# Forgetting attention and two MoE layers: one-bank PSUM tiles for the MoEs' outputs, and evictions issued one group earlier

## The chip, the cores and the metric

The kernel runs on one core of a Trainium2 chip. The metric is the device time of one execution in microseconds (us); lower is better.

## The reference

Attention with a decay over four batches of eight heads of 576 tokens, then two dense mixtures of the 2304 tokens (model width 512):

```python
scores = scale * q @ k.T + (cum[:, None] - cum[None, :])    # cum: running sum of log f, causal
x = softmax(scores) @ v                                      # 2304 tokens x 512
x = softplus(x @ w_in) @ w_out                               # first MoE, 2048 hidden
out = (sigmoid(x @ w_gate) * (x @ w_val)) @ w_out2           # second MoE, 1536 hidden
```

Every product is made in three matmuls of a high and a low part (high x high, high x low, low x high).

## The kernel before

The program has three stages, one behind the other, and PE (TensorE) works through all of them. Tiles are handed out by pools. An instruction waits for the instructions that used its tile, or the memory under it, before. The order on each engine is the order in which the code issues; nothing is reordered.

**Attention** (`Attention`, L22 on) works on 16 pairs of heads. A table of numbers (`WHEN`, `START`, `END`) sets the order. Scores go to PSUM banks `s` and to `X`; the products with v accumulate in two tiles of two banks each, `x_0` in `Y` and `x_1` in `X` (`pv`, L317). ACT (ScalarE) and DVE (VectorE) read them out: `out_a` (L340) and `out_b` (L345). In the last pair, `out_b` of `x_1` stands on DVE behind work on the first MoE's weights (`Weights.bits`, L502 to L506).

**The first MoE** (`Moe1`) takes five tiles of up to 512 tokens with 16 units each. `hidden` (L556 to L558 by the helper `three`) makes 12 matmuls into a bank `s`; ACT applies softplus (L586), ACT and DVE split the result into `gh` and `gl` (L597, L598). `output` adds 12 matmuls to four accumulators of one bank each. `BANKS` says where they lie: two of them in the `t` banks and two in a two-bank tile `Y`, or all four in `X` and `Y`. After the last unit of a tile `leave` (L625) copies the accumulators out, the even ones on DVE, the odd ones on ACT, and SP (SyncE) issues a DMA for each (L626). Those of the last tile are evicted while the second MoE begins.

**The second MoE** (`Moe2`) takes three tiles of 768 tokens with 12 units each. `hidden` makes seven products of six matmuls with 384 columns, into the two `s` banks `a` and `b` in turn; the third product needs the bank of the first one, so it waits until ACT has copied that out (L846, written `bl`). `output` adds 18 matmuls to six accumulators (blocks 0 to 5): blocks 0 and 1 in `t`, 2 and 3 in `X`, 4 and 5 in `Y`. On the last pass each finished block is evicted by `leave` (L916: even blocks DVE, odd blocks ACT) into a ring of four SBUF buffers `zs`, named `fw`, and SP issues its DMA to the output (L917). Block 4 so takes the buffer of block 0, and block 5 that of block 1; a copy into a buffer waits until the DMA out of it has landed. An eviction is not issued at once, but after the matmuls of the next block:

```python
            for x, y in self.leaves:
                self.leave(x, y)
            self.leaves = [(t, b)] if last else []
```

Block 5 of a tile is thereby issued after the first block of the next tile's first pass, one `hidden` later. The same unit's loads of weights stand on SP ahead of its DMA.

Of the kernel before, what the change touches and what calls it, by code (L numbers as in the profile page):

```python
# [21 lines left out]
class Attention:  # L22
# [2 lines left out]
    S = 576  # L25
    D = 64

    def __init__(self, nc, q, k, v, f, xT, pool, ps, dr):
        self.nc, self.q, self.k, self.v, self.f, self.xT = nc, q, k, v, f, xT
        self.B, self.HP = q.shape[0], q.shape[1]  # L30
        self.NP = self.B * self.HP
        self.c = pool("at_const", 1)
        self.R = {}
        self.ps, self.dr = ps, dr

    def pools(self, pool, io_pool):
        self.vp = pool("at_v", 2)
# [159 lines left out]
    def scores(self, R, p, i):  # L197


        nc, S = self.nc, self.S  # L200
        Xh, Xl, Yh, Yl, nb = R["Xh"], R["Xl"], R["Yh"], R["Yl"], self.nbs[p % 2]
        if "P" not in R:
            R["P"] = self.pp.tile([128, sum(self.W9)], F32, tag="P", name=f"P{p}")
            R["m"] = self.sm.tile([128, 9], F32, tag="m", name=f"m{p}")
            R["sum"] = self.sm.tile([128, 9], F32, tag="sum", name=f"sum{p}")
        n = 4
        if i == 4:
            ps = self.ps.tile([128, 1024], F32, tag="X", name=f"s{p}_4")
            for c in range(2):
                for j, (L, r) in enumerate(((Xh[:, 512:640], Yh), (Xl[:, 512:640], Yh), (Xh[:, 512:640], Yl),  # L210
                                            (self.one[:, 128:256], nb))):
                    nc.tensor.matmul(ps[:, 224 + 288 * c:512 + 288 * c], L, r[:, 288 * c:288 * c + 288],
                                     start=j == 0, stop=j == n - 1)
            R["src", 4] = R["P"], ps[:, 224:800], self.mask4
            return
        w = self.W9[i]
        N = max(w, 256)
        ps = [self.ps.tile([128, 512], F32, tag="s", bufs=2, name=f"s{p}_{i}_{h}") for h in range(2)]
        q = slice(128 * i, 128 * i + 128)
        for j, (L, r) in enumerate(((Xh[:, q], Yh), (Xl[:, q], Yh), (Xh[:, q], Yl), (self.one[:, 0:128], nb))):  # L220
            for h in range(2):
                o = slice(64 * h, 64 * h + 64)
                nc.tensor.matmul(ps[h][:, 0:N], L[o], r[o, 0:N], start=j == 0, stop=j == n - 1)  # L223
        for h in range(2):
            R["src", (i, 8 - i)[h]] = R["P"], ps[h][:, 0:w], self.mask[:, 512 - w:512]
# [94 lines left out]
    def pv(self, R, p, h, j):  # L320

        nc = self.nc
        if "acc%d" % h not in R:
            R["acc%d" % h] = self.ps.tile([128, 1024], F32, tag=("Y", "X")[h], name=f"x{p}_{h}")
        v = R["V"][:, j, h].rearrange("p a e -> p (a e)")
        for w in range(2):
            for tile, col, x, n in self.PV[h][j]:
                t = self.ptb[w] if tile == "b" else self.pta[p % 2][w]
                o = self.XO[h] + x
                nc.tensor.matmul(R["acc%d" % h][:, o:o + n], v, t[:, col:col + n], start=j == 0 and w == 0,  # L330
                                 stop=j == 1 and w == 1)
# [233 lines left out]
class Moe1:  # L565
# [35 lines left out]
    def output(self, u):  # L601
        nc = self.nc
        t, fc = divmod(u, self.FC)
        o, N = self.TILES[t]
        if fc == 0:

            self.acc[t] = []
            for b in self.BANKS[t]:
                if b == "t":
                    self.acc[t] += [self.ps.tile([128, 512], F32, tag="t", bufs=2, name=f"o{t}_{i}")[:, 0:N] for i in range(2)]  # L610
                else:
                    B = self.ps.tile([128, 1024], F32, tag=b, name=f"o{b}{t}")
                    self.acc[t] += [B[:, 0:N], B[:, 512:512 + N]]
        (wh, wl), (gh, gl) = self.W.done[f"wo{fc}"], self.g.pop(u)
        for d in range(4):
            three(nc, self.acc[t][d], [(block(wh, d), block(wl, d), gh, gl)], fc == 0, fc == self.FC - 1)
        if fc == self.FC - 1:
            for d in range(4):
                if d < 2 or t < self.NT - 1:
                    self.leave(t, d)  # L620
# [103 lines left out]
class Moe2:  # L724
# [3 lines left out]
    TILES = [(768 * i, 768) for i in range(3)]  # L728
    RING, OUTS = 3, 4

    def __init__(self, nc, FC, yT, out, S, chain, ps, slot, zs):
        self.nc, self.FC, self.yT, self.out, self.S, self.chain, self.ps = nc, FC, yT, out, S, chain, ps
        self.slot, self.zs, self.cache = slot, zs, {}
        self.NT, self.J = len(self.TILES), FC // 2
        self.n = self.NT * 2 * self.J
        self.acc, self.g, self.x, self.loaded = {}, {}, {}, 0
        self.early, self.late, self.leaves, self.z = [], [], [], 0

    def get(self, name, i):
        if (name, i) not in self.cache:  # L740
# [149 lines left out]
    def output(self, i, f):  # L890

        nc = self.nc
        t, j = divmod(i, self.J)
        first, last = (j, f) == (0, 1), (j, f) == (self.J - 1, 0)
        if first:
            T = [self.ps.tile([128, 512], F32, tag="t", bufs=2, name=f"zt{t}_{x}")[:] for x in range(2)]
            X, Y = (self.ps.tile([128, 1024], F32, tag=n, name=f"z{n}{t}") for n in "XY")
            self.acc[t] = T + [X[:, 0:512], X[:, 512:1024], Y[:, 0:512], Y[:, 512:1024]]
        w = 2 * ((2 * i + f) % self.OUTS)

        def piece(b):
            (h, l), a = self.g[i, f], self.acc[t][b]
            wh, wl = (self.get("w2", w + p) for p in range(2))
            gh, gl = block(h[b // 3], b % 3), block(l[b // 3], b % 3)
            nc.tensor.matmul(a, gh, wh, start=first, stop=False)
            nc.tensor.matmul(a, gh, wl, start=False, stop=False)
            nc.tensor.matmul(a, gl, wh, start=False, stop=last)
            for x, y in self.leaves:
                self.leave(x, y)
            self.leaves = [(t, b)] if last else []  # L910
        return [lambda b=b: piece(b) for b in range(6)]

    def leave(self, t, b):
# [12 lines left out]
    def run(self, first):  # L926
        for k in range(first, self.n):
            self.unit(k, self.output((k - 2) // 2, 1 - k % 2) if k > 1 else [])
        for f in self.early + self.late:
            f()  # L930
        for x in (1, 0):
            for f in self.output(self.n // 2 - 1, x):
                f()
        self.leave(*self.leaves[0])

# [15 lines left out]
def kernel(ctx: ExitStack, tc, q, k, v, f, w_in, w_out, w_gate, w_val, w2_out, out):  # L953
# [28 lines left out]
    with ExitStack() as actx:  # L982
        ioctx = ExitStack()
        right = pools(actx, side="right")
        at = Attention(nc, q, k, v, f, xT, right, ps, dr)
        at.pools(right, pools(ioctx, side="right"))
        at.begin()
        end = at.PERIOD * at.NP
# [13 lines left out]
        others += [(end + t, lambda u=u: m1[1].unit(u, 0)) for u, t in enumerate(UNITS)]  # L1002
        at.run(others)
    chain, m1 = m1
    xb = pool("xb", 1, **later)
    x1.pools.append(xb)
    wc = pool("wc", 1, **later)
# [66 lines left out]
            return xb_("hl"[i // 2])[:, 768 * (i % 2):768 * (i % 2) + 768]  # L1074
        return raw_(("G1", "V0", "V1").index(name) + 1).bitcast(F32)[:, 0:768]

    m2 = Moe2(nc, FC2, yT, out, S, buffers, ps, slot, ws)

    def pieces1(u):
        return 2 if u < FC1 else 0  # L1080
# [61 lines left out]
```

## Time and profile before

| | |
|---|---|
| median of 3 runs | 1032.04 us (1030.86 to 1032.93) |
| the profiled execution | 1032.53 us |
| its span, first to last instruction | 1030.7 us |
| PE busy | 1004.8 us (97%) |
| DVE, ACT, POOL busy | 616.2, 502.4, 152.8 us |
| granted TensorE clock, mean | 0.999 |

Times in the trace are counted from the start of the span. L556 is line 556 of the kernel before. A row of a timeline gives the start, the duration, the engine, the line, the operation, what it writes and reads, and in brackets how long the engine had idled and who released it. An engine's name with a q is its queue, which issues DMAs. The duration of one matmul covers its whole way through the array, so matmuls in a row overlap; how fast they follow each other is read from their starts.

### The profile page before, as it was taken

What the parts mean: (1) busy time and instruction counts of PE and PEld (TensorE: products, weight loads), DVE (VectorE), ACT (ScalarE), POOL (GpSimd) and SP (SyncE); (2) the same over time, 40 slices, a digit from 0 to 9 for tenths busy, and PEclk for the clock granted to TensorE, in tenths of its full rate; (3) what the DMA queues carried; (4) which work ended last, traced back from release to release, by engine and by line L of the source; (5) the groups of instructions that cost most, each with busy time, mean ns of one, the idle gap of its engine ahead of it and who ended that gap; (6) DMA issues with size and microseconds to landing.
All of it is one profiled execution on the core that took longest, in us unless ns stands there. A gap on an engine that the chain in (4) does not pass through costs nothing.

```text
span 1030.7 us, 15854 instructions
## 1 busy us (share of the span) xinstructions
PE 1004.8 (97%) x5584; PEld 881.4 (86%) x5584; DVE 616.2 (60%) x1238; ACT 502.4 (49%) x1069; POOL 152.8 (15%) x158
## 2 busy tenths in 40 slices
PE   5999999989999999999999999999999999999998
PEld 4788877868888889988888888999999999999997
DVE  4899999978955676745636644445344343443333
ACT  4888988866544445444334543333334333333332
POOL 7566777540000000000000000000000000000000
PEclk9999999999999999999999999999999999999999
DMA  5354554445635656627525766775678666676641
GB/s 148 108 146 129 167 158 126 138 148 179 210 122 194 217 198 245 249 85 260 194 102 185 256 243 242 258 245 184 217 245 274 215 211 223 210 245 215 218 139 61
DMA packets 114698, 196.07 MB, mean 190 GB/s; under 512 B 14702, under 2 KB 38398, under 8 KB 114620
## 3 DMA queue, kind: packets, MB, share of 16 engines
q1 hardware_dynamic: 112684, 189.98, 55.2%
q10 hardware_dynamic: 1936, 5.09, 1.6%
q8 instruction: 44, 0.72, 0.3%
q14 instruction: 34, 0.28, 0.1%
HBM read 149.19 MB, written 45.83 MB: 189 GB/s over the span
## 4 chain that ended last, share of the span: by engine, by line
PE 91%; DVE 5%; ACT 2%; DMA 1%; issue 1%; SPq 0%; ACTq 0%; DVEq 0%
PE z L556 8%; PE z L558 8%; PE z L557 8%; PE h L556 6%; PE h L557 6%; PE h L558 6%; PE s L223 5%; PE x L330 4%; PE t L254 4%; PE oY L556 2%; PE oY L558 2%; PE oY L557 2%; PE o L557 2%; PE o L558 2%; PE o L556 2%; PE oX L556 2%
## 5 line engine op out<-in xcount | busy, mean ns | idle before, releaser
L556 PE MATMUL z<-three,three 128*128 128x384 f32 x456 | 153.2, 336 | 1.6 <-ACT u L854 1.2
L558 PE MATMUL z<-three,three 128*128 128x384 f32 x456 | 152.9, 335 | 0.0
L557 PE MATMUL z<-three,three 128*128 128x384 f32 x456 | 152.6, 335 | 0.0
L586 ACT ACTIVATE L<-h 128x512 f32<-128x512 f32 (+1 forms) x80 | 44.3, 554 | 156.1 <-PE h L558 156.0
L598 DVE TENSOR_TENSOR gl<-L,gh 128x512 fp32r<-128x512 f32 (+1 forms) x80 | 51.1, 638 | 110.5 <-ACT gh L597 109.4
L556 PEld LDWEIGHTS z<-three,three 128*128 128x128 f32 x456 | 85.6, 188 | 4.1 <-ACT u L854 1.5
L235 ACT ACTIVATE P<-P,m 128x128 f32<-128x128 f32 (+3 forms) x144 | 83.1, 580 | 10.7 <-DVE m L230 10.5
L557 PEld LDWEIGHTS z<-three,three 128*128 128x128 f32 x456 | 85.6, 188 | 1.4
L558 PEld LDWEIGHTS z<-three,three 128*128 128x128 f32 x456 | 85.6, 188 | 0.0
L230 DVE CUSTOM_DVE_ANT_0 P<-s,mask 128x256 f32<-128x256 f32 (+3 forms) x144 | 70.6, 516 | 11.2 <-PE s L223 6.4
L280 DVE TENSOR_TENSOR PTl<-t,PTh 128x512 fp32r<-128x512 f32 (+2 forms) x112 | 66.8, 619 | 6.0 <-ACT PTh L276 5.8
L254 PE MATMUL t<-ident,P 128*128 128x128 f32 x400 | 61.3, 287 | 7.3 <-DVE PTl L280 5.7
L858 DVE TENSOR_TENSOR raw<-z,bh 128x384 f32<-128x384 f32 x36 | 20.1, 558 | 77.9 <-PE z L558 77.9
L851 DVE TENSOR_TENSOR raw<-z,p 128x384 f32<-128x384 f32 x18 | 10.0, 558 | 93.5 <-PE z L558 79.6
L276 ACT CAST PTh<-t 128x512 fp32r<-128x512 f32 (+2 forms) x112 | 56.3, 536 | 18.2 <-PE t L254 17.7
L846 ACT COPY bl<-z 128x384 f32<-128x384 f32 x36 | 17.3, 481 | 96.4 <-PE z L558 96.4
L254 PEld LDWEIGHTS t<-ident,P 128*128 128x128 f32 x400 | 44.6, 144 | 21.3 <-DVE PTl L280 7.0
L880 ACT CAST gh<-raw 128x384 fp32r<-128x384 f32 x72 | 33.6, 514 | 48.6 <-DVE raw L863 47.2
L330 PE MATMUL x<-PTh,V 128*128 128x256 f32 (+2 forms) x224 | 56.4, 312 | 0.0
L330 PE MATMUL x<-PTl,V 128*128 128x256 f32 (+2 forms) x224 | 54.4, 293 | 0.0
L700 DVE TENSOR_TENSOR l<-fw,sh 128x512 fp32r<-128x512 f32 x60 | 40.7, 686 | 14.1 <-ACT sh L699 11.8
L597 ACT CAST gh<-L 128x512 fp32r<-128x512 f32 (+1 forms) x80 | 46.3, 578 | 2.6
(284 smaller groups left out, 2651.0 us busy)
## 6 DMA issues: line engine op xcount, KB each, us to landing
three<-sd_g SPq DMA_DIRECT2D x126, 256.0 KB
three<-sd_v SPq DMA_DIRECT2D x126, 256.0 KB
two<-sd_w SPq DMA_DIRECT2D x36, 256.0 KB
raw_wi<-in_moe_w_in_dram SPq DMA_DIRECT2D x16, 512.0 KB
raw_wo<-in_moe_w_out_dram SPq DMA_DIRECT2D x16, 512.0 KB
fraw<-in_moe_w_gate_dram SPq DMA_DIRECT2D x12, 512.0 KB
fraw<-in_moe_w_out_dram SPq DMA_DIRECT2D x12, 512.0 KB
sd_g<-sh SPq DMA_DIRECT2D x24, 256.0 KB
```

What stands on the lines that cost most here:

```text
L223: nc.tensor.matmul(ps[h][:, 0:N], L[o], r[o, 0:N], start=j == 0, stop=j == n - 1)
L230: self.nc.vector.tensor_tensor_reduce(P, src, mask, -0.125, 3e38, op0=ALU.add, op1=ALU.min, accum_out=R["m"][:, t:t + 1])
L235: self.nc.scalar.activation(P, P, AF.Exp, bias=R["m"][:, t:t + 1], scale=-1.0, accum_out=R["sum"][:, t:t + 1])
L254: nc.tensor.transpose(ps[:, 128 * n:128 * n + 128], R["P"][:, o:o + 128], self.ident)
L276: self.nc.scalar.copy(d, s)
L280: self.nc.vector.tensor_sub(l, s, h)
L330: nc.tensor.matmul(R["acc%d" % h][:, o:o + n], v, t[:, col:col + n], start=j == 0 and w == 0, stop=j == 1 and w == 1)
L556: nc.tensor.matmul(ps, ah, bh, start=start and i == 0, stop=False, **how)
L557: nc.tensor.matmul(ps, ah, bl, start=False, stop=False, **how)
L558: nc.tensor.matmul(ps, al, bh, start=False, stop=stop and i == n - 1, **how)
L597: nc.scalar.copy(gh, s)
L598: nc.vector.tensor_sub(gl, s, gh)
```

## The change

The accumulators of both MoEs that lay two by two in the two-bank tiles `X` and `Y` become four tiles of one bank (`X0`, `X1`, `Y0`, `Y1`) in a pool `four`. Attention keeps its two-bank tiles in a pool `wide`, which is closed when attention ends; `four` is opened on the same four banks after it. `Moe2.output` calls `leave` right after a block's own last matmul, so that the list `leaves` and the call at the end of `run` go away.

```diff
-            ps = self.ps.tile([128, 1024], F32, tag="X", name=f"s{p}_4")
+            ps = self.wide.tile([128, 1024], F32, tag="X", name=f"s{p}_4")
...
-            R["acc%d" % h] = self.ps.tile([128, 1024], F32, tag=("Y", "X")[h], name=f"x{p}_{h}")
+            R["acc%d" % h] = self.wide.tile([128, 1024], F32, tag=("Y", "X")[h], name=f"x{p}_{h}")
...
-                    B = self.ps.tile([128, 1024], F32, tag=b, name=f"o{b}{t}")
-                    self.acc[t] += [B[:, 0:N], B[:, 512:512 + N]]
+                    self.acc[t] += [self.four.tile([128, 512], F32, tag=f"{b}{i}", name=f"o{b}{t}_{i}")[:, 0:N] for i in range(2)]
...
-            X, Y = (self.ps.tile([128, 1024], F32, tag=n, name=f"z{n}{t}") for n in "XY")
-            self.acc[t] = T + [X[:, 0:512], X[:, 512:1024], Y[:, 0:512], Y[:, 512:1024]]
+            self.acc[t] = T + [self.four.tile([128, 512], F32, tag=n, name=f"z{n}{t}")[:] for n in ("X0", "X1", "Y0", "Y1")]
...
-            for x, y in self.leaves:
-                self.leave(x, y)
-            self.leaves = [(t, b)] if last else []
+            if last:
+                self.leave(t, b)
...
-        self.leave(*self.leaves[0])
...
+        wide = actx.enter_context(tc.tile_pool(name="wide", bufs=1, space=PSUM))
+        at = Attention(nc, q, k, v, f, xT, right, ps, wide, dr)
...
+    four = m1.four = pool("four", 1, space=PSUM, **later)
```

The order on PE, DVE and POOL stays as it was. On ACT and SP block 5 of the first two tiles of `Moe2` moves; elsewhere only waits change. Three places follow. In the rows `waits` names the engine, or the DMA lane (DMAHW), whose semaphore a row waits for.

The first place is PE, where the first unit's `output` of the first MoE opens its accumulators (`o_0`, `o_1` in the `t` banks, then `oY`). Before:

```order
L556 MATMUL o_0_3392<-gh_3308,wi_h 128x512 [waits PE_49,Activation_49]
L557 MATMUL o_0_3392<-gl_3309,wi_h 128x512 [waits DVE_49]
L558 MATMUL o_0_3392<-gh_3308,wo_l 128x512
L556 MATMUL o_1_3393<-gh_3308,wi_h 128x512 [waits PE_49]
L557 MATMUL o_1_3393<-gl_3309,wi_h 128x512
L558 MATMUL o_1_3393<-gh_3308,wo_l 128x512
L556 MATMUL oY_3394<-gh_3308,wi_h 128x512 [waits PE_49]
```

Now:

```order
L556 MATMUL o_0_3399<-gh_3311,wi_h 128x512 [waits PE_49,Activation_49]
L557 MATMUL o_0_3399<-gl_3312,wi_h 128x512 [waits DVE_49]
L558 MATMUL o_0_3399<-gh_3311,wo_l 128x512
L556 MATMUL o_1_3400<-gh_3311,wi_h 128x512 [waits PE_49]
L557 MATMUL o_1_3400<-gl_3312,wi_h 128x512
L558 MATMUL o_1_3400<-gh_3311,wo_l 128x512
L556 MATMUL oY_0_3401<-gh_3311,wi_h 128x512 [waits DVE_49,Activation_49]
```

DVE's order at that place, which is the same before and now (`gl` is what the row of `o_0` above waits for, `x_0` and `x_1` are attention's accumulators of the last pair):

```order
L345 TENSOR_TENSOR xs_3285<-x_0_3226,bs_3286 64x576 [waits DMAHW4_49,DMAHW3_49,DMAHW5_49,Activation_49,Pool_49]
L598 TENSOR_TENSOR gl_3309<-L_3306,gh_3308 128x512 [waits Activation_49]
L502 TENSOR_SCALAR w_wo_3313<-w_wo_3313 128x512 [waits Activation_49]
L504 SCALAR_TENSOR_TENSOR w_wo_3313<-raw_wo_3241,w_wo_3313 128x512 [waits DMAHW3_49,DVE_49]
L506 SCALAR_TENSOR_TENSOR w_wo_3313<-raw_wo_3241,w_wo_3313 128x512 [waits DVE_49]
L345 TENSOR_TENSOR xs_3285<-x_1_3243,bs_3286 64x576 [waits PE_49]
```

The pool `four` gives its first tile, `Y0`, the banks that held attention's `X`. Before, `oY` lay on the banks of `x_0` and had nothing left to wait for on DVE; now `oY_0` lies on those of `x_1` and waits for the last row here.

The second place is ACT at the end of the second MoE's first tile (`fw_4053` and `fw_4061` are the buffer of block 1, `z` without a letter are the `s` banks). Before:

```order
L916 COPY fw_4053<-zt_1_6906 128x512 [waits PE_49]
L916 COPY fw_4055<-zX_6907 128x512 [waits DMAHW7_49,DVE_49]
L846 COPY bl<-z_6753 128x384 [waits PE_49,Activation_49]
L848 COPY p_6751<-z_6754 128x384 [waits PE_49,Activation_49]
L880 CAST gh_6_8020<-raw_6816 128x384
L880 CAST gh_6_8021<-raw_6816 128x384
L854 COPY u_6752<-z_6754 128x384 [waits PE_49,Activation_49]
L856 COPY bh<-z_6753 128x384 [waits PE_49,Activation_49]
L861 ACTIVATE raw_6750<-raw_6750 128x768 [waits DVE_49]
L868 ACTIVATE bl<-bl 128x768 [waits DVE_49]
L788 CAST three_6315<-bh 128x768 [waits DMAHW6_49]
L916 COPY fw_4053<-zY_6908 128x512 [waits DMAHW0_49,Activation_49]
```

Now:

```order
L914 COPY fw_4061<-zt_1_6920 128x512 [waits PE_49]
L914 COPY fw_4063<-zX_6922 128x512 [waits DMAHW7_49,PE_49]
L914 COPY fw_4061<-zY_6924 128x512 [waits DMAHW0_49,PE_49,Activation_49]
L846 COPY bl<-z_6767 128x384 [waits PE_49]
L848 COPY p_6765<-z_6768 128x384 [waits PE_49]
L880 CAST gh_6_8040<-raw_6830 128x384 [waits DVE_49]
```

Block 5's copy has moved from behind the next unit's work to ahead of it, and keeps its wait for the DMA out of block 1's buffer (DMAHW0). Block 3's copy waits for PE instead of DVE. The end of the second tile reads the same.

The third place is ACT where the first MoE's last tile is evicted inside the second MoE's third unit. Before:

```order
L625 COPY fw_4053<-oX_6112 128x512 [waits DVE_49]
L846 COPY bl<-z_6753 128x384 [waits PE_49,Activation_49]
L848 COPY p_6751<-z_6754 128x384 [waits PE_49,Activation_49]
L880 CAST gh_0_6923<-raw_6816 128x384
L880 CAST gh_0_6924<-raw_6816 128x384
L625 COPY fw_4055<-oY_6113 128x512 [waits DVE_49]
L854 COPY u_6752<-z_6754 128x384 [waits PE_49,Activation_49]
```

Now:

```order
L624 COPY fw_4061<-oX_1_6125 128x512 [waits PE_49]
L846 COPY bl<-z_6767 128x384 [waits PE_49,Activation_49]
L848 COPY p_6765<-z_6768 128x384 [waits PE_49,Activation_49]
L880 CAST gh_0_6939<-raw_6830 128x384 [waits DVE_49]
L880 CAST gh_0_6940<-raw_6830 128x384
L624 COPY fw_4063<-oY_1_6127 128x512
L854 COPY u_6766<-z_6768 128x384 [waits PE_49,Activation_49]
```

Nothing has moved there; the two evictions on ACT no longer wait for DVE's copy of the other half.

## Rows read from the trace of the kernel before

**Rows 1.** The page: busy time, share of the span, instructions.

```profile
PE 1004.8 (97%) x5584; PEld 881.4 (86%) x5584; DVE 616.2 (60%) x1238; ACT 502.4 (49%) x1069; POOL 152.8 (15%) x158
```

**Rows 2.** Waits of PE from 231 us on, all: total, times, longest (us).

```profile
PE z L556 <- ACT u L854: 1.2, 1, 1.2
PE z L556 <- ACT bl L846: 0.3, 1, 0.3
PE zY L905 <- ACT fw L916: 0.2, 1, 0.2
```

**Rows 3.** Timeline of PE at the first MoE's first two outputs.

```profile
223.55 0.39 PE L556 MATMUL oY<-gh,wi_h 128*128 128x512 f32 x1
223.78 0.39 PE L557 MATMUL oY<-gl,wi_h 128*128 128x512 f32 x1
...
227.63 0.47 PE L556 MATMUL o<-gh,wo_h 128*128 128x512 f32 x1
228.37 0.50 PE L557 MATMUL o<-gl,wo_h 128*128 128x512 f32 x1 [0.28 <-DVE gl L598]
```

**Rows 4.** Timeline of DVE at the same time.

```profile
224.08 1.67 DVE L506 SCALAR_TENSOR_TENSOR w_wo<-raw_wo,w_wo 128x512 uint32<-128x512 uint32 x1
225.77 0.76 DVE L345 TENSOR_TENSOR xs<-x,bs 64x576 f32<-64x576 f32 x1
```

**Rows 5.** Timelines of PE and ACT where the first MoE's last tile is evicted.

```profile
628.74 0.34 PE L558 MATMUL z<-three,three 128*128 128x384 f32 x1
629.34 0.44 PE L556 MATMUL z<-three,three 128*128 128x384 f32 x1 [0.26 <-ACT bl L846]
...
632.39 0.34 PE L558 MATMUL z<-three,three 128*128 128x384 f32 x1
633.89 0.44 PE L556 MATMUL z<-three,three 128*128 128x384 f32 x1 [1.16 <-ACT u L854]
...
628.32 0.59 ACT L625 COPY fw<-oX 128x512 f32<-128x512 f32 x1 [2.07 <-DVE fw L625]
...
632.87 0.59 ACT L625 COPY fw<-oY 128x512 f32<-128x512 f32 x1 [2.38 <-DVE fw L625]
```

**Rows 6.** Timelines of SP, DVE, ACT and PE around the second MoE's first tile end.

```profile
766.24 0.34 SPq L917 DMA_DIRECT2D out_dram<-fw  x1
...
766.68 0.51 SPq L917 DMA_DIRECT2D out_dram<-fw  x1
...
768.42 0.69 DVE L916 COPY fw<-zY 128x512 f32<-128x512 f32 x1 [1.60 <-PE z L558]
...
767.41 0.48 ACT L846 COPY bl<-z 128x384 f32<-128x384 f32 x1
...
768.03 0.33 PE L558 MATMUL z<-three,three 128*128 128x384 f32 x1
768.20 0.33 PE L556 MATMUL z<-y1h,three 128*128 128x384 f32 x1
...
775.97 0.39 PE L907 MATMUL zX<-raw,gl 128*128 128x512 f32 x1
776.56 0.50 PE L905 MATMUL zY<-raw,gh 128*128 128x512 f32 x1 [0.20 <-ACT fw L916]
```

**Rows 7.** The same for the second tile's end: SP (block 1), PE.

```profile
904.39 0.38 SPq L917 DMA_DIRECT2D out_dram<-fw  x1
...
905.91 0.33 PE L556 MATMUL z<-three,three 128*128 128x384 f32 x1
```

**Rows 8.** Timelines at the end: SP (block 1), PE's last matmul, ACT's last copy.

```profile
1024.34 0.34 SPq L917 DMA_DIRECT2D out_dram<-fw  x1
...
1026.02 0.39 PE L907 MATMUL zY<-three,gl 128*128 128x512 f32 x1
...
1027.21 0.59 ACT L916 COPY fw<-zY 128x512 f32<-128x512 f32 x1 [0.82 <-DVE fw L916]
```

**Rows 9.** Busy time by stretch, the last 1.4 us (PEclk: granted clock).

```profile
1029.30:1030.70 1.40, 0.00 (x0) 0.00 (x0) 0.00 (x0) 0.00 (x0) 0.00 (x0) 0.50 0.06 22
```

More of the change, by code (lines that the diff above doesn't have):

```diff
@@ L26, with __init__ @@
     D = 64
-    def __init__(self, nc, q, k, v, f, xT, pool, ps, dr):
+    def __init__(self, nc, q, k, v, f, xT, pool, ps, wide, dr):
         self.nc, self.q, self.k, self.v, self.f, self.xT = nc, q, k, v, f, xT
@@ L33, in __init__ @@
         self.R = {}
-        self.ps, self.dr = ps, dr
+        self.ps, self.wide, self.dr = ps, wide, dr
     def pools(self, pool, io_pool):
@@ L729, with __init__ @@
     RING, OUTS = 3, 4
-    def __init__(self, nc, FC, yT, out, S, chain, ps, slot, zs):
+    def __init__(self, nc, FC, yT, out, S, chain, ps, four, slot, zs):
+        self.four = four
         self.nc, self.FC, self.yT, self.out, self.S, self.chain, self.ps = nc, FC, yT, out, S, chain, ps
@@ L736, in __init__ @@
         self.acc, self.g, self.x, self.loaded = {}, {}, {}, 0
-        self.early, self.late, self.leaves, self.z = [], [], [], 0
+        self.early, self.late, self.z = [], [], 0
     def get(self, name, i):
@@ L984 @@
         right = pools(actx, side="right")
-        at = Attention(nc, q, k, v, f, xT, right, ps, dr)
+        wide = actx.enter_context(tc.tile_pool(name="wide", bufs=1, space=PSUM))
+        at = Attention(nc, q, k, v, f, xT, right, ps, wide, dr)
         at.pools(right, pools(ioctx, side="right"))
@@ L1075, in buffers @@
         return raw_(("G1", "V0", "V1").index(name) + 1).bitcast(F32)[:, 0:768]
-    m2 = Moe2(nc, FC2, yT, out, S, buffers, ps, slot, ws)
+    m2 = Moe2(nc, FC2, yT, out, S, buffers, ps, four, slot, ws)
     def pieces1(u):
```

## The prediction

> **What bounds the kernel now.** I read the busy times first: PE is busy 97% of the span [rows 1]. So the question is only where PE stands still, and the list of PE's waits answers it: from 231 us on there are three, all short, all on ACT [rows 2]. Everything else DVE, ACT and the DMAs do is hidden, and any microsecond by which PE is held up or let go in the MoEs goes straight into the time. I then read the timelines around four places where the change alters a wait: the first MoE's first output, the change-over from the first MoE to the second, the ends of the second MoE's first two tiles, and the end of the program. Elsewhere the change alters waits too (the ends of the first MoE's first four tiles), but there PE has no wait now that could go, and the copies only come earlier; I cost these at nothing, covered by the 12 hidden matmuls that PE does between two tiles.
>
> An ordinary 512-column matmul follows the one before by 0.23 us [rows 3], a 384-column one by 0.17 us [rows 6].
>
> **Term 1, the first output: +2.5 us.** By the order, the first matmul into `oY_0` now waits for attention's last `out_b` on DVE. In the trace that one stands behind a weight operation of 1.67 us and runs from 225.77 to 226.53 [rows 4]. PE reached the matmul at 223.55 [rows 3], so it is late by 2.98. PE's sequencer is in order, so everything queued behind the matmul is late as well. One later wait is swallowed: at the second output PE now stands from 227.63 to 228.37 in place of 0.23, a loss of 0.51, for a `gl` that will be long there when PE comes three microseconds later [rows 3]. Net 2.98 - 0.51 = +2.47. What comes next on ACT and DVE (softplus of the third hidden group, then weight work) moves with PE and has no PE wait behind it today, so I see nothing that gives it back. From both sides: the weight operation is the one thing in front that could be shorter, and the nearest row for that is the `out_b` behind it, 0.76 [rows 4]; so 0.9 less, +1.6, and +3.0 if the second output's wait stayed.
>
> **Term 2, the change-over: -1.8 us.** Here ACT stands 2.07 and 2.38 us for DVE's copies of the other half of a two-bank tile [rows 5], and PE's two largest waits [rows 2] hang on the ACT copies behind: matmul starts 0.60 apart (628.74 to 629.34) and 1.50 apart (632.39 to 633.89) in place of 0.17, so 0.43 + 1.33 = 1.76 lost. With tiles of one bank ACT's evictions wait for PE alone, whose accumulators are done before; ACT can do each in the idle time shown, 0.59 long. Both PE waits go. What is late next is the ordinary copy of the bank behind its own product, which PE does not wait for in other units. From both sides: at least the idle times themselves, 0.26 + 1.16 = 1.42; at most 2.0, with the slow restarts (the matmul after each stall follows later than 0.17).
>
> **Term 3, the ends of the first and second tile: +1.7 and +1.7 us, less 0.4.** The earlier issue brings block 5's copy ahead of the next unit's copies on ACT, and it keeps its wait: its buffer is block 1's, whose DMA must have landed. That wait was covered before, since the copy came some 7 us later. How long does the DMA take? DVE's copy of block 4 waits in the same way for block 0's DMA; it is issued at 766.24 and the copy starts at 768.42, 2.18 us later [rows 6]. (The row names PE as releaser. But two products of six matmuls, 2.1 us, stand between the last matmul on block 4 and the third product at 768.20, so the block was done by about 766.1, and I take the releaser to be the DMA.) Block 1's DMA is issued at 766.68, behind block 0's on SP, so I expect it to be there at 768.86. Then ACT copies block 5 (0.59, as its other evictions) and only then `bl` (0.48), ready at 769.93; PE wants that bank for the third product at 768.20 [rows 6]. PE is late by 1.73. Behind the waiting copy ACT queues `p`, the two casts and `u`; they have the slack of PE's own delay. On SP, block 5's DMA now stands ahead of nine loads of weights, which are delayed by about the same; those fill a ring of three units of (904.39 - 766.68) / 12 = 11.5 us each [rows 6, 7], and PE waits for no load today [rows 2], so they stay covered. At the second tile the pattern repeats: issued at 904.39, there at 906.57, `bl` ready at 907.64 against 905.91 [rows 7]: +1.73. What the earlier issue removes is PE's wait for block 5's late copy at 776.56, starts 0.59 apart in place of 0.23: -0.36 [rows 6]. The second tile has no such wait. From both sides, each new wait: if the landing took 1.6 us, +1.1; if 2.8, +2.3.
>
> **Term 4, the end: -0.7 us.** The last matmul starts at 1026.02 and is done at 1026.41; ACT's last copy starts at 1027.21, behind DVE's copy of block 4 [rows 8]. Now it needs PE and the landing of block 1's DMA, issued at 1024.34 [rows 8]: 1024.34 + 2.18 = 1026.52. So 0.69 earlier, and the last DMA with it; between 0 and 0.8.
>
> **The sum** is 2.47 - 1.76 + 1.73 + 1.73 - 0.36 - 0.69 = +3.1 us. The profiled execution took 1032.53 us, so its like would take 1035.6; the median of the runs lies 0.5 lower, so I forecast 1032.04 + 3.1 = 1035.2 us. All lower ends together give about +0.7, all upper ones about +6. Independent terms hardly meet at one end: +1.2 to +5.6 is what I keep, 1033.2 to 1037.6.
>
> **Rival 1: the ring does not hold ACT (not slower).** If block 5's copy did not have to wait for block 1's DMA, ACT would do it right after PE, before `bl` is wanted, and both +1.73 would go: 3.1 - 3.5 = -0.4, 1031.7 us. It decides by whether that DMA has landed when PE finishes the first product, about one product (1.0 us) before 768.20. For it: the row names PE, not a DMA. Against it: the DMA is not even issued before 766.68, and DVE idles 1.60 with its input done.
>
> **Rival 2: PE does not wait at the first output.** If attention's last `out_b` were done by 223.55, term 1 would go: 3.1 - 2.5 = +0.6, 1032.7 us. Against it is DVE's order, which the change leaves alone, and a finish 3 us too late [rows 4].
>
> **Rival 3: the clock.** Term 1 makes PE stand for nearly 3 us. In the only stretch of the rows in which the granted clock is at its lower level, 1.2 GHz (0.50), PE had done nothing since its last matmul was over at 1026.41 [rows 8, 9]; the stalls of up to 1.2 us [rows 2] did not lower it. If it fell here, each 512-column matmul would take 0.46 in place of 0.23; for one unit's 24 matmuls that is 5.5 us, for half of one 2.8. I take 4: 1039 us. For it: the new stall is longer than any the trace shows the clock to outlast. Against it: PE is busy right before and after. On the same point the Trainium skill's "TensorE: Matmul & The Clock Gate", section "Part 1: The HAM clock gate", says that the slow clock is the default state and that activity of PE releases it, so standing still is what puts it back; by that rule the new wait could cost more than its length, and the last row agrees, with 0.50. Whether a stall of this length is enough, no row shows.
>
> **How the numbers follow.** 0.2% of the time, about what a measurement of this kernel can tell from no change, is 2.1 us. My forecast has 0.70, rival 1 has 0.06, rival 2 has 0.08, rival 3 has 0.12, and 0.04 is left for both new waits being absent, 3.1 - 3.5 - 2.5 = -2.9, 1029.1 us. Rivals 1 and 2 are within 0.2%; of my forecast's own range some 0.06 is too. So faster 0.04, same 0.20, slower 0.76. Range 1033.2 to 1037.8: it leaves out rival 1, rival 2, most of rival 3 and the last case, a little under 0.2 with what they overlap.
>
> **What would show each step.** Term 1: in the list of PE's waits a new one of about 3 us of `oY` on DVE's L345, and no more wait of the second output for `gl`. Term 2: the two waits at 629 and 634 us gone, and ACT's copies of `oX` and `oY` released by PE. Term 3: two new waits of PE's third product on `bl`, 1.5 to 2 us each, with ACT's block 5 copy right ahead of it idling before; no wait at `zY`. Term 4: the last ACT copy 0.1 us after the last matmul. I am wrong if PE's wait at `oY` is missing or under 1 us, if block 5's copy follows block 3's without a pause, or if the granted clock falls anywhere before the end.

## The result and the profile after

| | median | runs | span of the profiled execution |
|---|---|---|---|
| before | 1032.38 us | 1030.79 to 1033.27 | 1030.7 us |
| after | 1039.13 us | 1038.12 to 1040.51 | 1037.8 us |

The changed kernel is slower by 0.7%: the ratio is 1.0068, its 95% interval 1.0055 to 1.0081. The median moved by 6.75 us, the span by 7.1; forecast were 3.1.

Both kernels make the same 5584 matmuls in the same order, so the start of each can be set against its start before. How late PE is (start after less start before) changes at eight places:

| place | start before | start after | lateness |
|---|---|---|---|
| first output, `oY` | 223.55 | 226.67 | 0.0 to 3.1 |
| the ten matmuls from there | | | 3.1 to 4.8 |
| second output, wait for `gl` gone | | | 4.8 to 4.2 |
| change-over, the two waits gone | 629.34, 633.89 | 633.21, 636.33 | 4.3 to 2.3 |
| end of the first tile of the second MoE | 768.20 | 772.42 | 2.2 to 4.3 |
| the matmuls from there | | | 4.3 to 5.9 |
| `zY` wait gone | 776.56 | 782.06 | 5.9 to 5.4 |
| end of the second tile | 905.91 | 913.15 | 5.3 to 7.35 |

The last matmul is 7.5 us late (1026.02 to 1033.53, [rows 8]), the span 7.1.

PE's list of waits from 200 us on (total, times, longest; the last three belong to attention's end and the first units and stand in the trace of before too) has two new ones on top, against the three of [rows 2]:

```profile
PE z L556 <- ACT bl L846: 3.6, 2, 1.9
PE oY L556 <- DVE xs L345: 2.9, 1, 2.9
PE t L254 <- DVE PTl L280: 2.3, 2, 1.3
PE rt L292 <- DVE PTl L280: 0.8, 1, 0.8
PE o L556 <- ACT gh L597: 0.5, 1, 0.5
```

The first output in the timelines of PE and DVE, as in [rows 3, 4]. `out_b` (L345) ends at 226.5, behind the weight operation, and PE goes on then. Look at the starts after the wait: they lie 0.30, 0.35 and then 0.43 apart up to 230.3, in place of 0.23, then 0.23 again.

```profile
223.34 0.39 PE L558 MATMUL o<-gh,wo_l 128*128 128x512 f32 x1
226.67 0.47 PE L556 MATMUL oY<-gh,wi_h 128*128 128x512 f32 x1 [2.94 <-DVE xs L345]
226.97 0.55 PE L557 MATMUL oY<-gl,wi_h 128*128 128x512 f32 x1
...
227.74 0.63 PE L556 MATMUL oY<-gh,wi_h 128*128 128x512 f32 x1
228.17 0.63 PE L557 MATMUL oY<-gl,wi_h 128*128 128x512 f32 x1
...
230.61 0.39 PE L557 MATMUL h<-xl,wo_h 128*128 128x512 f32 x1
230.84 0.39 PE L558 MATMUL h<-xh,wi_l 128*128 128x512 f32 x1
...
224.09 1.63 DVE L506 SCALAR_TENSOR_TENSOR w_wo<-raw_wo,w_wo 128x512 uint32<-128x512 uint32 x1
225.76 0.76 DVE L345 TENSOR_TENSOR xs<-x,bs 64x576 f32<-64x576 f32 x1
```

Why they lie further apart stands in the view by stretches (stretch, its length, busy us and instructions of PE, weight loads, DVE, ACT and POOL, then the granted clock, the DMAs' share and GB/s), first around the first output, then around the ends of the two tiles:

```profile
222.00:232.00 10.00, 6.83 (x23) 5.13 (x23) 4.51 (x6) 4.25 (x8) 4.84 (x3) 0.83 0.33 114
767.00:779.00 12.00, 10.14 (x48) 9.59 (x47) 4.67 (x10) 3.72 (x8) 0.00 (x0) 0.86 0.91 317
904.00:916.00 12.00, 10.27 (x53) 9.21 (x53) 7.66 (x13) 4.63 (x10) 0.00 (x0) 1.00 0.66 237
```

In the kernel before the granted clock is 1.00 in all three. Here it fell to its lower level, 1.2 GHz (0.50), behind the wait of 2.94 us and again behind the one of 1.86, and stayed there for about 3.4 us each time (0.17 of 10 us and 0.14 of 12 are lost, at half speed). ("Behind" a wait is in the profiles of this case from 0.5 us before its end to 1.3 us after it.) It did not fall behind the third, 1.73 us long.

The ends of the two tiles, on ACT and PE, as in [rows 6, 7]: ACT stands 3.68 and 3.55 us for the DMA out of block 1's buffer, copies block 5, then `bl`, and PE waits for that.

```profile
771.40 0.59 ACT L914 COPY fw<-zY 128x512 f32<-128x512 f32 x1 [3.68 <-DMA out_dram<-fw]
771.88 0.48 ACT L846 COPY bl<-z 128x384 f32<-128x384 f32 x1
...
772.42 0.44 PE L556 MATMUL z<-y1h,three 128*128 128x384 f32 x1 [1.86 <-ACT bl L846]
...
912.13 0.59 ACT L914 COPY fw<-zY 128x512 f32<-128x512 f32 x1 [3.55 <-DMA out_dram<-fw]
912.62 0.48 ACT L846 COPY bl<-z 128x384 f32<-128x384 f32 x1
...
913.15 0.44 PE L556 MATMUL z<-three,three 128*128 128x384 f32 x1 [1.73 <-ACT bl L846]
```

At the change-over (against [rows 5]) ACT makes both copies without a pause, and the matmuls that stood 0.60 and 1.50 apart now stand 0.17 apart. At the end (against [rows 8]) ACT's last copy starts 0.22 us after the last matmul, which ends at 1033.92. From the start of that matmul to the end of the span pass 4.28 us, before 4.73.

```profile
630.48 0.59 ACT L624 COPY fw<-oX 128x512 f32<-128x512 f32 x1
...
634.67 0.59 ACT L624 COPY fw<-oY 128x512 f32<-128x512 f32 x1
...
633.04 0.33 PE L558 MATMUL z<-three,three 128*128 128x384 f32 x1
633.21 0.33 PE L556 MATMUL z<-three,three 128*128 128x384 f32 x1
...
1033.53 0.39 PE L906 MATMUL zY<-three,gl 128*128 128x512 f32 x1
...
1034.14 0.59 ACT L914 COPY fw<-zY 128x512 f32<-128x512 f32 x1 [0.96 <-DMA out_dram<-fw]
```

### The profile page after: what moved, and what is told of

The parts are those of the page before. It is cut to its first block, busy times and chain, and to the rows that moved or that the text cites. A ratio compares the mean times of both kernels' runs of the same rounds, so it can differ in the third digit from the quotient of the medians.

```text
span 1037.8 us, 15852 instructions
## 1 busy us (share of the span) xinstructions
PE 1007.6 (97%) x5584; PEld 884.2 (85%) x5584; DVE 617.4 (59%) x1238; ACT 502.5 (48%) x1069; POOL 152.8 (15%) x158
## 4 chain that ended last, share of the span: by engine, by line
PE 91%; DVE 5%; ACT 2%; DMA 1%; issue 1%; SPq 0%; ACTq 0%; DVEq 0%
PE z L556 8%; PE z L558 8%; PE z L557 8%; PE h L558 6%; PE h L556 6%; PE h L557 6%; PE s L223 5%; PE x L330 4%; PE t L254 4%; PE oY L557 3%; PE oY L558 3%; PE oY L556 3%; PE o L558 2%; PE o L556 2%; PE o L557 2%; PE oX L558 2%
```

## The experiments

Theory A: each wait adds its own length to PE's lateness, and the granted clock falls because PE stood still. The rivals put the loss elsewhere (VectorE's backlog, the four tiles as such) or tie the clock to the place in the program. All ratios are against the kernel before on the same chip.

### The pool split (twice)

```diff
-        wide = actx.enter_context(tc.tile_pool(name="wide", bufs=1, space=PSUM))
+        wide = {n: actx.enter_context(tc.tile_pool(name="wide" + n, bufs=1, space=PSUM)) for n in "YX"}
```

> The changed kernel, with attention's pool split in two pools, opened Y first, so that the four new tiles Y0 and Y1 take the banks of the accumulator that attention frees first (as before the change). Theory A (each wait adds its length to PE, and the granted clock falls after the long ones): the 2.9 us wait of PE at the first matmul of oY0 goes, with it the fall of the clock at 227 us; the 0.5 to 0.6 us wait for gl at the second output returns. The changed kernel's 1039.1 less 3.1 less 1.7 plus 0.6 is 1034.9 us. The waits of about 1.8 us at the ends of the first two tiles of the second MoE stay, at about 768 and 907 us; if the clock doesn't fall behind them this time, 1033.3. Rival B (the wait comes from VectorE being behind with its work there, whichever bank is taken): the wait stays and the time is 1039. Rival C (the two falls of the clock belong to the places in the program, not to the waits): the fall near 224 us stays, 1036.5.

> The split pool once more (evictions issued at once), for a second profile and more times. All theories: no wait at the first output, waits of 1.7 to 2.0 us at the ends of the first two tiles. Theory A with the counts so far (behind a wait of 2.8 us or more the clock fell each time, behind 1.8 to 2.0 us in two of four profiles, behind 1.7 us in none of five): 1033.7 us within 0.7, with the fall behind the first of the two waits in about half of the executions, none behind the second, none near 224 us.

Measured: 1033.73 us, 1.0012 (1.0004 to 1.0021), and 1034.06 us, 1.0019 (1.0010 to 1.0028). The wait at the first output is gone. The ring's two waits stay, 1.91 and 1.74 us, in the second profile 1.83 and 1.74. The clock fell behind none of them, nor near 224 us; the three stretches of the first profile:

```profile
222.00:232.00 10.00, 9.73 (x43) 7.60 (x42) 6.66 (x11) 6.29 (x11) 4.88 (x3) 1.00 0.34 108
767.00:779.00 12.00, 10.97 (x57) 10.23 (x58) 5.14 (x10) 5.63 (x11) 0.00 (x0) 1.00 0.77 265
904.00:916.00 12.00, 10.27 (x54) 9.36 (x53) 3.71 (x7) 4.71 (x9) 0.00 (x0) 1.00 0.93 327
```

So the first output's wait comes from the bank that `oY_0` is given: theory A's number without a fall, 1033.3, and not rival B's 1039. VectorE's order is that of the changed kernel. Rival C's fall at 224 us did not come.

### Late evictions with four tiles (twice)

```diff
-            if last:
-                self.leave(t, b)
+            for x, y in self.leaves:
+                self.leave(x, y)
+            self.leaves = [(t, b)] if last else []
```

> The changed kernel, with the evictions issued a group later again, as before the change; the four tiles and the pools stay. Theory A: the first output's wait of 2.9 us and the fall of the clock at 227 us stay, and the gain of 2.0 us at the change-over stays; the waits of 1.9 and 1.7 us of PE on ACT's block 5 at the ends of the first two tiles go, and the fall of the clock at 773 us with them, the wait of 0.5 us before zY returns: 1039.1 less 2.1 less 1.6 less 2.0 plus 0.5, and the end 0.6 longer, is 1034.5 us. Rival B (it is the four tiles, not the order of issue, that hold ACT at the ring of out buffers): the two waits stay, 1039. Rival C (the falls of the clock belong to the places in the program): the fall near 771 us stays without a wait, 1036.

> The late evictions with the four tiles once more, for a second profile and more times. Theory A: the wait of 2.9 us at the first output again, and the clock falls behind it again, as in each of the four profiles with that wait; nothing behind 230 us until the end; the time of the run without two DMAs (1033.6) less what the DMAs' absence and the end give there, so 1033 to 1034 us. Rival E (falls come by chance, in these four by luck): no fall near 227 us, 1032 us.

Measured: 1032.88 us, 1.0004 (0.9995 to 1.0013), and 1033.36 us, 1.0006 (0.9998 to 1.0015). No wait on the ring, and the clock is 1.00 there; the first output is as in the changed kernel, its wait 2.93 us and the clock's fall behind it in both profiles. The second one:

```profile
226.80 0.77 PE L556 MATMUL oY<-gh,wi_h 128*128 128x512 f32 x1 [2.93 <-DVE xs L345]
...
222.00:232.00 10.00, 6.84 (x22) 5.05 (x22) 4.63 (x6) 4.38 (x8) 4.82 (x3) 0.83 0.34 113
767.00:779.00 12.00, 12.00 (x65) 11.14 (x64) 6.49 (x12) 6.12 (x11) 0.00 (x0) 1.00 0.85 293
```

It is the order of issue that holds ACT at the ring, not the four tiles. The times are 1.6 and 1.1 us below the 1034.5 of theory A. Of that, 0.6 is the end, which the theory took to be as before. ACT's last copy starts 0.61 us after the start of the last matmul (1027.32 against 1026.71 in the first profile), as in the changed kernel, and not 1.19 as in the kernel before; so the gain at the end comes with the four tiles. In the two profiles PE needs 1.9 and 1.7 us more than in the kernel before from its first `o` matmul to its last; theory A's terms there are 3.1 + 1.7 - 0.6 - 2.0 = 2.2. Why the medians lie another 1.0 and 0.5 below the theory is open; the first is about what its interval allows, 0.9 to either side.

### Both repairs: the fastest kernel

```diff
-            if last:
+            for x, y in self.leaves:
+                self.leave(x, y)
+            hold = last and b == 5 and t < self.NT - 1
+            self.leaves = [(t, b)] if hold else []
+            if last and not hold:
                 self.leave(t, b)
```

with the split pool.

> Both edits at once, the second one cut down: attention's pool split as in the first run, and of the evictions only block 5 of the first two tiles is issued a group later; all others are issued at once. Theory A: no wait at the first output, none on block 5, no fall of the clock; what is left are the change-over's 2.0 us, 0.5 us before zY and 0.6 us at the end, all gains: the kernel before, 1032.4, less 3.1, is 1029.3 us, faster than both. Rival B (the gain of the change-over was only time made up, because PE came there 4 us late and so found its copies done): without the lateness the change-over's waits return and the time is 1031.3 or more. Rival C (the falls of the clock belong to the places): 1032.6.

Measured: 1029.39 us, 0.997 (0.996 to 0.998) of the kernel before. PE has no wait left between 231 and 1030 us, and the clock is 1.00 in all three stretches. The change-over's gain was not time made up: at 640 us PE is 1.97 us earlier against the kernel before than at 627, with no lateness ahead of it. This version beats both kernels.

### Matmuls in place of the first wait

```diff
+        if u == 0:
+            for _ in range(12):
+                nc.tensor.matmul(self.acc[0][0], block(wh, 0), gh, start=True, stop=True)
         for d in range(4):
```

> The changed kernel, with twelve more matmuls at the first output, ahead of its first block (they write the first block's tile, which the next matmul starts anew, so the result is that of the kernel without them). At 0.23 us each they take 2.8 us, about as long as the wait before oY0. Theory A (the clock fell because PE stood still): PE works in the time in which it waited; the wait before oY0 is under 0.3 us, the clock stays at 1.0 near 227 us, and the time is the changed kernel's 1039.1 less 1.7, so 1037.4 us, though PE has more work. Rival C (the fall belongs to the place or to attention's end): the clock falls near 227 us all the same, 1039. Rival D (the wait is not for a thing done at a fixed time, but follows PE): the wait stays behind the twelve matmuls, 1042.

Measured: 1038.85 us, 1.0057 (1.0044 to 1.0070), so 1.4 above theory A. The profile holds its first half: the wait is 0.7 us, the clock stays at 1.00, and with 2.7 us more work PE is at 600 us 1.24 us *earlier* than in the changed kernel. Of that gain 0.33 us is left at 780 us: the wait on the ring is 2.80 us in place of 1.86, with the clock's fall behind it:

```profile
222.00:232.00 10.00, 9.25 (x41) 7.31 (x41) 4.42 (x6) 5.10 (x10) 4.87 (x3) 1.00 0.33 109
767.00:779.00 12.00, 9.20 (x44) 8.87 (x43) 3.72 (x8) 3.13 (x7) 0.00 (x0) 0.86 0.86 306
...
772.08 0.44 PE L556 MATMUL z<-y1h,three 128*128 128x384 f32 x1 [2.80 <-ACT bl L849]
```

### The changed kernel again, and matmuls in place of all three waits

The second of these adds, to the twelve matmuls above, at the starts of the second and third tile:

```diff
+        if t and r == 2:
+            for _ in range(11):
+                nc.tensor.matmul(b, block(A["A11"][0], 0), B["x11"][0][0], start=True, stop=True, skip_group_check=True)
         product(b, "A11", "x11", True)
```

> The changed kernel itself once more, so that the next three stand beside it on the same chip, and for a second profile of it. All theories: 1039.1 us within 0.7. Theory A (each of the three long waits of PE makes the granted clock fall, or nearly each): the clock falls behind at least two of the waits near 224, 771 and 912 us. Theory E (a wait of this length makes the clock fall in some executions and not in others): other places than 227 and 773 us in this profile, and runs that lie up to 3.5 us apart.

> The changed kernel with matmuls in place of all three waits: the twelve ahead of the first output's first block, and eleven more ahead of the product for which PE stood ready when it waited for ACT's block 5, at the starts of the second and the third tile (they write the bank that the product's first matmul starts anew). 12 by 0.23 and 11 by 0.17 us make 2.7, 1.9 and 1.9 us, the lengths of the waits. Theory A (PE stands still, so the clock falls): no fall between 200 and 1020 us, waits under 1 us each, the time 1039.1 less 1.7 less 1.6, so 1035.8 us. Theory E (the falls come in some executions only; their mean cost is what the first call leaves unexplained when the waits' costs are added, 1039.1 less 1033.7 less 1032.9 plus 1029.4 plus 0.6 for the end, 2.5 us): 1036.6. Rival C (the falls belong to the places, or the sum fails for another reason): 1039.

Measured: the changed kernel 1039.55 us, 1.0061 (1.0048 to 1.0074). In this profile the clock fell behind the first of the three waits and not behind the second, of 1.84 us, nor the third, and the span is 1036.2, 1.6 less than 1037.8. Theory A's falls behind at least two of the three did not come: a wait near 2 us lowers the clock in some executions and not in others. The filled kernel took 1038.83 us, 1.0060 (1.0046 to 1.0074), 3 us above theory A's 1035.8. The clock falls nowhere between 222 us and the last matmul, but the rest of the theory misses. The clock was low from 208 to 215 us, ahead of all the edits, where the expectation had no fall (the last section shows this stretch). And behind the added matmuls PE still waits 0.60 and 1.18 us, since ACT's wait for block 1's buffer grew from 3.68 and 3.55 us to 4.33 and 4.91. The DMA queues between the end of ACT's copy of block 1 and the start of that of block 5 at the second tile (packets, MB, share of 16 engines) show in the filled kernel a packet of instruction code that the changed kernel has not there:

```profile
q1 hardware_dynamic: 544, 1.02, 46.6%
q8 instruction: 1, 0.02, 1.2%
```

What that does is told at the end. As a test of the clock's cost the two runs with added matmuls are inconclusive, because something else moved with the added code.

### Without the DMAs of blocks 0 and 1

```diff
-        nc.sync.dma_start(self.out[o:o + 128, :], z)
+        if b > 1 or t == self.NT - 1:
+            nc.sync.dma_start(self.out[o:o + 128, :], z)
```

> The changed kernel without the DMAs that carry blocks 0 and 1 of the first two tiles of the second MoE to the output (those 512 rows stay unwritten; all else is computed). Theory A (block 5's copy on ACT waits for the DMA that empties block 1's buffer): ACT's waits of 3.6 us are gone, block 5 leaves as soon as its last matmul ends, PE's two waits of 1.9 and 1.7 us and the clock's fall behind the first go, the wait before zY returns: 1039.1 less 2.1, 2.0 and 1.6, plus 0.5, is 1033.9 us. Rival F (ACT is held there by other things of the row, its own six copies in a row, and the DMA is only the last of them): the waits shrink by under a half and the time is 1037 or more.

Measured: 1033.60 us, 1.0008 (0.9999 to 1.0017), theory A's 1033.9. ACT's copy of block 5 is now released by PE and starts 1.4 us after that of block 3:

```profile
766.91 0.59 ACT L914 COPY fw<-zX 128x512 f32<-128x512 f32 x1 [0.24 <-PE zX L906]
768.32 0.59 ACT L914 COPY fw<-zY 128x512 f32<-128x512 f32 x1 [0.83 <-PE zY L906]
769.33 0.48 ACT L846 COPY bl<-z 128x384 f32<-128x384 f32 x1 [0.42 <-PE z L558]
```

PE has no wait there, and the clock stays at 1.00. So it is the DMA that holds ACT, and not the other things of its row (rival F).

### VectorE's last piece moved ahead

```diff
-        ("out_a", 1): 68.1148, ("out_b", 1): 69.4238, ("out_c",): 86.9253, ("out_d",): 99.8167}
+        ("out_a", 1): 68.1148, ("out_b", 1): 68.3, ("out_c",): 86.9253, ("out_d",): 99.8167}
```

> The changed kernel, banks as they are, but with VectorE's last piece of attention's accumulator X moved ahead of the weights' bit operations in the order of the end of attention. Theory A (Y0 takes the banks of X, which that piece frees, and the piece stands late in VectorE's queue): the wait of 2.9 us before oY0 goes, and with it the fall of the clock: as in the split pool's run, 1033.7 us, to 1034.9. Rival B (VectorE has no time to spare there: what is moved forward moves something else back, the parts gl or the weights that the first units need): PE waits 2 to 3 us for gl or for weights in place of oY0, 1038 to 1039.

Measured: 1035.14 us, 1.0025 (1.0015 to 1.0035). The wait at `oY_0` is gone with the banks as they are, and the clock is 1.00 there, so the wait is the piece's place on VectorE times the bank, and either repairs it. Behind the ring's first wait, 1.95 us, the clock fell in this profile, which is theory A's 1034.9.

### The early issue alone

The kernel before, with `leave` called at once and its two-bank tiles kept.

> The kernel before, with one part of the change alone: evictions issued at once, not a group later; the accumulators stay two tiles of two banks. Theory A (the ring of four out buffers holds ACT's block 5 whatever the tiles are): PE waits 1.7 to 2.0 us for ACT at the starts of the second and the third tile, 2.1 and 2.0 us with the start of the matmuls behind it; the wait before zY and the end give back 0.5 and 0.6; the waits at the change-over stay as before; no long wait at the first output. 1032.5 plus 3.0 is 1035.5 us, and 1037.1 where the granted clock falls behind the first of the two waits. Rival B (it takes the four tiles for the waits to appear): 1032 to 1032.5.

Measured: 1044.98 us, 1.0123 (1.0109 to 1.0137), slower than every other and outside both theories. PE waits one block earlier than either had it:

```profile
766.72 0.79 PE L905 MATMUL zX<-three,gh 128*128 128x512 f32 x1 [2.64 <-DVE fw L915]
...
770.43 0.50 PE L905 MATMUL zY<-three,gh 128*128 128x512 f32 x1 [0.79 <-DVE fw L915]
...
909.17 0.51 PE L905 MATMUL zX<-three,gh 128*128 128x512 f32 x1 [2.64 <-DVE fw L915]
...
905.00:919.00 14.00, 10.58 (x39) 8.61 (x38) 5.27 (x10) 4.37 (x9) 0.00 (x0) 0.76 0.53 178
```

Blocks 2 and 3 are the two halves of one tile. With block 2's eviction issued ahead of block 3's matmuls, these wait for DVE's copy of the other half, and the same for blocks 4 and 5. The late issue was what kept two-bank tiles free of this wait, and with the four tiles the early issue doesn't bring it. The clock fell behind both waits of 2.64 us, the second time for about 6.8 us (0.24 of 14 us lost, at half speed), twice as long as behind the other waits. All six waits on DVE's copies, those of the last tile included, make 8.5 us, the clock's two falls about 5 (an estimate from those times at half speed); the span is 12.9 us longer. The ring's wait was not reached in this run, so it says nothing on it.

### The same instructions in another order

```diff
-        for d in range(4):
-            three(nc, self.acc[t][d], [(block(wh, d), block(wl, d), gh, gl)], fc == 0, fc == self.FC - 1)
+        part = lambda ds: [three(nc, self.acc[t][d], [(block(wh, d), block(wl, d), gh, gl)], fc == 0, fc == self.FC - 1) for d in ds]
+        if u == 0:
+            part((0, 1))
+            self.rest = lambda: part((2, 3))
+        else:
+            part(range(4))
...
+                if done == 1:
+                    self.rest()
```

> The changed kernel, banks and evictions as they are, with the same instructions in another order at one place: blocks 2 and 3 of the first output, which wait for attention's last piece, come behind the third unit's twelve matmuls into h and not ahead of them. Those take 2.7 us, so PE has its own later work in the time of the wait, and no code is added (in the two runs with added matmuls a load of instruction code lay beside the out DMA that ACT waits for, and that wait was 0.6 to 1.3 us longer). Theory A: the wait before oY0 shrinks from 2.9 to under 0.4 us, no fall of the clock near 227 us; the 0.5 us wait for gl returns, the two waits on the ring stay at 1.7 to 1.9 us: 1039.4 less 3.1, less 1.6, plus 0.6, is 1035.3 us, and 1033.9 as with the split pool where the clock doesn't fall behind the ring's first wait. Rival B (the work that is moved forward meets a wait of its own, for the weights of its unit or the bank of h): a wait of over 1 us at the moved matmuls, 1037 or more.

Measured: 1033.47 us, 1.0012 (1.0003 to 1.0021). With the twelve matmuls of `h` in its time the wait is 0.24 us, and the clock stays at 1.00:

```profile
226.52 0.47 PE L556 MATMUL oY<-gh,wi_h 128*128 128x512 f32 x1 [0.24 <-DVE xs L345]
...
222.00:232.00 10.00, 9.63 (x41) 7.49 (x42) 6.66 (x11) 6.31 (x12) 4.89 (x3) 1.00 0.32 111
767.00:779.00 12.00, 10.29 (x53) 9.22 (x53) 5.66 (x10) 5.44 (x10) 0.00 (x0) 1.00 0.86 300
```

PE makes the first matmul of the second output 4.45 us earlier than in the changed kernel: 2.7 of the wait, some 1.6 for the clock, and 0.2 by which this execution was ahead before. The ring's waits are there (1.71 and 1.74 us), without a fall.

## Why the prediction was wrong

The direction and all four terms held; the sum was too small by what the clock took, 3.2 us, and by 0.3 to 0.4 for each wait at the ring.

| step | forecast | measured on PE, or at the end |
|---|---|---|
| Term 1, wait less what the second output regains | +2.47 | 3.10 - 0.63 = +2.47 |
| Term 2, change-over | -1.76 | -1.96 |
| Term 3, the two ring waits | +1.73, +1.73 | +2.13, +2.01 |
| Term 3, `zY` | -0.36 | -0.48 |
| Term 4, end | -0.69 | -0.45 (-0.58 at ACT's copy) |
| sum of the terms | +3.1 | +3.7 |
| granted clock | 0 | 1.68 + 1.56 = +3.2 |

Together that is 6.9 of the 7.1 us by which the span grew.

**Term 1** was right in place, cause and size: DVE's L345 stands behind the same weight operation (1.63), the split pool, the moved piece and the moved matmuls each take the wait away, and nothing later gave it back.

**Term 2** was right, and no lateness was needed for it: the kernel with both repairs has it too. Its 0.2 more is the restart of the matmuls, inside the bounds given.

**Term 3** was right in its mechanism (the run without the DMAs shows it) and 0.3 to 0.4 too low per wait. The mis-sized step is the landing of block 1's DMA, put at 2.18 us after its issue from block 0's: with PE 2.20 late, that is 768.86 + 2.20 = 771.06, but ACT's copy started at 771.40. From issue to copy passed 2.52 us (from 768.88) and at the second tile 2.39 (909.74 to 912.13). The slower restart of the matmuls made up the rest.

**Term 4** was right to 0.1 at ACT's copy; the end of the span gained 0.45 of it.

**What failed is the clock, which the sum put at nothing and rival 3 held for unlikely**, in three ways. Its chance of 0.12 was too low: the argument against it, that PE is busy right before and after, does not hold, and of five profiles with the 2.9 us wait the clock fell in all five. It was priced for Term 1 alone, though Term 3's waits are stalls too, and longer than the 1.2 us that the trace of before showed the clock to outlast; the wait of 1.86 us brought the second fall. And the price of one fall, 4 us, was too high: about 3.4 us at the lower level cost 1.6. Two falls made 3.2, near the 4 of the rival by two errors against each other. The time of the rival, 1039, is close to what was measured; the forecast put the range's upper end, 1037.8 (its own sum gives 1037.6), below it. The Trainium skill's "TensorE: Matmul & The Clock Gate", section "Part 1: The HAM clock gate", was quoted for saying that the slow clock is the default and PE's activity releases it. The trace agrees: where PE's own later work stood in the time of the wait, the clock stayed up at the same place of the program.

Rivals 1 and 2 fell: ACT stood 3.68 us for the DMA, and the wait of `oY` came.

One thing stays open. With the first times of the three kernels, the two parts' costs add up to 1033.73 + 1032.88 - 1029.39 = 1037.2 us, 1.9 below the changed kernel. By the widths of the four intervals such a sum is good to about 2 us (an estimate), so this may be chance. In the first profiles of the three, none of which has a fall of the clock at the ring, the parts add up: from PE's first `o` matmul to its last pass 805.8 us with the split pool, 806.3 with the late evictions and 802.1 with both, which makes 810.0. The changed kernel takes 809.9 in the profile without that fall and 811.9 in the one with it (before: 804.5). If most of its executions have the fall and few of the split pool's do, that is the difference; two profiles of each don't show how often it comes.

## What to carry to other kernels

When a pool is split or reopened, ask which memory each new tile is given and who still has to read it: here the first output lost 3.1 us to the wait and 1.7 to the clock behind it, and opening two pools in another order removed both. Before an eviction is issued sooner, look for the wait that the later place had been covering: the buffer's DMA on ACT, and the other half of a shared tile on PE. Count a new stall of a TensorE that was nearly always busy twice: its length, and the slower matmuls behind it. In the changed kernel these cost 1.6 to 1.7 us for each fall of the clock, and over all profiles the fall came behind every wait near 3 us and behind 2 of 13 near 2 us.

## What the runs showed of the hardware that was not expected

**The clock and the length of a wait.** Over all profiles of this case, behind waits of PE of 2.64 to 2.94 us the granted clock fell 8 times of 8. Behind waits of 1.71 to 1.95 us it fell 2 times of 13: in the changed kernel (1.86) and with VectorE's piece moved (1.95), while 1.91, 1.84 and 1.83 us passed without.

Several shorter waits in a row brought a fall too. At the end of attention, ahead of every wait that the edits alter, PE waits 1.30, 0.83 and 0.34 us and then 0.97 or 0.55, all within 6 us and in each of the 14 profiles, and the clock fell there in 6 of them. In the changed kernel's first profile it is 1.00 over this stretch; its second profile and the filled kernel's show

```profile
204.00:218.00 14.00, 10.53 (x63) 9.03 (x62) 10.65 (x19) 7.80 (x18) 6.43 (x6) 0.88 0.55 158
204.00:218.00 14.00, 10.96 (x55) 9.46 (x54) 11.13 (x19) 7.47 (x16) 5.82 (x5) 0.76 0.54 158
```

From the wait of 1.30 us to the first `o` PE takes 14.8 us without the fall, 15.2 to 15.7 with it, and 16.5 in the filled kernel, where the clock was low twice as long. So in these profiles neither the length of one wait nor the place decides alone, and executions of one kernel can differ by this time ahead of everything that the edits alter.

**Instruction code beside an output DMA.** From the end of ACT's copy of block 1 to the start of block 5's, which waits for block 1's DMA, 4.35 to 4.60 us pass at 13 of the 16 tile ends in the eight profiles with the four tiles, the early issue and all DMAs. At the three others, all in the two kernels with added matmuls, it was 5.16, 5.44 and 5.77; these three are the only ones in which a packet of 0.02 MB of the queue q8, instruction code, moved in that time. A smaller packet, 0.01 MB of instruction code on q14, moved at the first tile's end in seven of the eight; where it was alone 4.48 to 4.60 us passed, and 4.35 to 4.43 where no code moved. So added instructions may lengthen a transfer far behind them. That the packet is the cause is inferred from its coming with each of the three; it was not tried by itself.
